# Two attentions in one kernel: the agenda of A's softmax and of B's output weights is rewritten

## The chip, the core and the metric

The kernel runs on one core of a Trainium2 chip. The metric is the device time of one launch in microseconds (us). Before the change three runs took 1605.85, 1606.92 and 1607.03 us; their median, 1606.92, is the time that is compared.

## The reference

Two attention layers work on inputs of 2048 positions by 576 features with 32 heads of 18, in float32, and their outputs are joined along the features.

```python
# A: every position looks at 8 positions, 2 apart, at and behind itself
logits = jnp.einsum("bhsd,bhswd->bhsw", q, kg) * scale
logits = jnp.where(mask, logits, -1e9)
o = jnp.einsum("bhsw,bhswd->bhsd", softmax(logits), vg)
# B: full attention
scores = jnp.einsum("bhqd,bhkd->bhqk", q, k) * scale
o = jnp.einsum("bhqk,bhkd->bhqd", softmax(scores), v)
# both: qkv = x @ wqkv before, o @ wo after
```

## The kernel before

**Stages.** A first part (to about 415 us) projects the inputs with split operands (each float32 number as a high and a low half). Then comes the main loop: B's attention in 512 *steps*, `while step < ALL` (L1272). A step takes one group `g` of four heads, one block `b` of 512 queries and one tile `kt` of 128 keys; 16 steps make a block, 64 a group. Blocks are numbered through, so block 30 is `g` 7, `b` 2 and begins at step 480.

**What a step does.** TensorE (PE) makes four score products (L269), ScalarE (ACT) four exponentials `e` (L277), and PE weighs the values by the exponentials of the step before into `po` (L742, eight matmuls together in a trace, four to a step and two row sets). Beside that PE makes *maximum pieces* for later blocks (L158), score products again, whose row maxima VectorE (DVE) takes (L166): three of them in a step. They go through three PSUM banks in turn, so PE can be at most three pieces ahead of DVE. When a block's 64 pieces are done, DVE reduces and turns them (L176, L183), GpSimd (POOL) splits them into two halves (`halve`, L101 and L102), and `place` (L195) has eight small DMAs write the rows into the tile `qs`, from which the block's own scores are made. A block's first score needs its rows.

**The agenda.** Everything else hangs on a table from steps to closures: `plan(start, ...)` and `later(n, f)` put work on a step, and `due()` issues it, in order, at the end of the step. What is issued is bound to its engine's queue in that order: DVE, POOL and ACT, and SP, which issues nearly all the DMAs, each work strictly through their own queue, so an instruction that waits holds what is behind it.

**A's part.** A is cut into eight pieces `j` of 256 positions; `AT[j]` is the step to which the plan of piece `j` refers (L43, `local`, L891). POOL multiplies queries with shifted keys and adds (`match`, nine times, the last at `AT+25`, which ends in `lg`, L921). DVE takes the maximum over the window (`most`, L932 into `am`, at `AT+31`, 32, 33), POOL subtracts it (`lower`, L938), ACT makes the exponentials (`exponents`, L941, at `AT+35`), DVE adds them (`total`, L932 into `as`, at `AT+36`, 37, 38) and takes reciprocals (`inverses`, L948, at `AT+38` and 39), POOL multiplies (`share`, L951, at `AT+39`) and makes nine weighted sums (`weighted`, L957 to L960, `AT+39` to `AT+59`). The result is split (L964, L969) and stored to `dao` (L972). For the first piece all from `most` on lies three steps earlier. `get` loads it back (L987, L989).

**Double steps.** A's output products for a half tile (288 columns) are put into `inside` at the steps of the table `MADE` (L45). If one stands there when a step with `kt > 0` begins, `together` (L1227) runs two steps as one: eight scores, eight maximum pieces and A's products interleaved over two halves of the array. `due()` for the first of the two is called only after all of this is issued, `due()` for the second after the weighing. There are 32 entries; each stands for one double step that begins one step after it.

**B's results.** When a block is weighed, `finish` (L747) copies `po`, loads its sums of 16 by 128 into `den` one step later, takes their reciprocal (L786) eight steps later, stores it (L787) nine steps later, loads it spread out as `rec` (L788) at 13, multiplies, casts and subtracts on POOL at 20, 21, 22 (L789 to L791) and stores at 26 (L777). The last group has a shorter table.

**B's output weights.** `load_wo` (L849) loads a chunk of rows into a buffer `y` (four buffers, shared with A's outputs), and six steps later POOL splits it into tiles of group 5, free from step 384 on (L101, L102). Chunks 0 to 4 start at steps 455, 457, 459, 461 and 463. The fifth has four pieces of 18 rows and a POOL memset first. `load_wo_stack` (L872) does the like for two stacked pieces at steps 465 and 467, and nine steps later copies rows by DMA (L886). `fetch_old` (L1038) loads 8 transfers of 252 KB: B's results of the seven finished groups for a block of queries, for block 0 at step 452 and for block 1 at step 472.

Of the kernel before, what the change touches and what calls it, by code (L numbers as in the profile page):

```python
# [16 lines left out]
S = 2048  # L17
D = 576
H = 32
DH = 18  # L20
# [19 lines left out]
EARLY_PAIRS = EARLY * NB * PIECES + 2  # L40
AHEAD = 7

AT = [10, 67] + [13 + 55 * j for j in range(2, S // AB)]  # L43

MADE = ((88, 96, 112, 128), (144, 160, 176, 192), (200, 208, 224, 240), (253, 256, 272, 288),  # L45
        (307, 320, 336, 352), (362, 368, 384, 400), (417, 432, 440, 448), (474, 476, 478, 480))


def ap(t, *dims):
# [4 lines left out]
def rows(t, *dims):  # L54

    return bass.AP(tensor=t.tensor, offset=t.offset, ap=[list(d) for d in dims])
# [3 lines left out]
def two_attentions(ctx: ExitStack, tc, xa, wa, woa, xb, wb, wob, out):  # L60
# [686 lines left out]
    def finish(g, b):  # L747
        o = work.tile([128, 512], F32, name="o", bufs=2)
        if g == NG - 1 and b == NB - 1:
            return closing(b, o, work.tile([128, 512], F32, name="rec", bufs=1))  # L750
        if step + 1 in producing and total - sum(given) >= 8:
            leaving.append(lambda: nc.scalar.activation(o, po, AF.Copy))
        elif step + 1 in producing or sum(given) == total:
            nc.scalar.activation(o, po, AF.Copy)
        else:

            nc.vector.tensor_copy(o, po)
            copied.add(step + 1)
# [12 lines left out]

        if g == NG - 1 and b > 0:
            return shortly(b, o, rec, *room())

        def store():
            if g < NG - 1:
                load(do[:, g, :, 512 * b : 512 * b + 512].rearrange("i p n -> p i n"), parts[2].bitcast(F32))  # L777
            else:
                for i in range(2):
                    load(do[i, g, :, 512 * b : 512 * b + 512], parts[i].bitcast(F32))  # L780
                later(2, lambda: stack_new(b))
                plan(step + 2, full(b))

        times = (1, 8, 9, 13, 20, 21, 22, 26) if g < NG - 1 else (1, 6, 7, 10, 13, 14, 15, 16)
        for at, f in zip(times, (lambda: load(den, o[DH:128:32]),
                                 lambda: nc.vector.reciprocal(den, den),  # L786
                                 lambda: load(drec[g, b].rearrange("i (p n) -> (i p) n", n=16), den),  # L787
                                 lambda: load(rec, rows(drec[g, b], (512, 4), (0, 32), (1, 512))),  # L788
                                 lambda: nc.gpsimd.tensor_mul(o, o, rec),  # L789
                                 lambda: nc.gpsimd.tensor_copy(room()[0], o),  # L790
                                 lambda: nc.gpsimd.tensor_sub(parts[1], o, parts[0]),  # L791
                                 store)):
            later(at, f)
# [52 lines left out]
    producing = set()  # L846
    copied = set()

    def load_wo(k, src, *pieces):  # L849

        raw = work.tile([128, D], F32, name="y", bufs=4)
        n = 0
        if len(pieces) == 4:
            nc.gpsimd.memset(raw, 0.0)
            n = 128
        for at, c0, m in pieces:
            load(raw[at : at + m], src[c0 : c0 + m])
            n = max(n, at + m)
        if k == "a":
            hi = work.tile([128, D], F32R, name="wohi", bufs=5)  # L860
            lo = work.tile([128, D], F32R, name="wolo", bufs=5)
        else:

            c = len(wo.get(k, []))
            hi, lo = (ap(t[:, 0, 0, :] if len(t.shape) == 4 else t[:, 0, :], (1, NB * 1024))[:, D * c : D * c + D]
                      for t in sets[(NG - 3) % 3])
        wo.setdefault(k, []).append((hi, lo))
        later(3 if k == "a" else 6, lambda: split_on(nc.gpsimd, hi[:n], lo[:n], raw[:n]))

    wstack = []  # L870
# [1 line left out]
    def load_wo_stack(p):  # L872

        hi, lo = (ap(t[:, 0, 0, :] if len(t.shape) == 4 else t[:, 0, :], (1, NB * 1024))[:, D * (5 + p) : D * (6 + p)]
                  for t in sets[(NG - 3) % 3])
        raw = work.tile([128, D], F32, name="y", bufs=4)
        nc.gpsimd.memset(raw, 0.0)
        for r in range(2):
            load(raw[64 * r : 64 * r + 3 * DH], rows(wob[DH * (H - 4 + r + 2 * p)], (0, 3), (D, DH), (1, D)))
        wstack.append(hi)  # L880
        later(6, lambda: split_on(nc.gpsimd, hi[:118], lo[:118], raw[:118]))

        def middle():
            for r in range(2):
                at = slice(64 * r + DH, 64 * r + 2 * DH)
                load(hi.bitcast(F32)[at], lo.bitcast(F32)[at])  # L886

        later(9, middle)


    def local(j):  # L891
# [104 lines left out]
            for_two.add(inside[-1])  # L996

        def sums_of_a(h, n, alone=True):
            his, los = zip(*wo["a"])
            w = his[:4], los[:4], his[4], los[4]  # L1000
            cols = slice(288 * h, 288 * h + 288)
            if h == 0:
                st["y"] = ys["a", j, n] = work.tile([128, D], F32, name="y", bufs=4)
            y = st["y"][:, cols]
            both = [halves(r, 0, w, st["x", n], cols, slice(0, 128), True) for r in range(2)]
            if not alone:
                return both, y
            one, two = beside("scores", *both)
            nc.scalar.activation(y, two, AF.Copy)
            behind_scores.append(lambda: nc.vector.tensor_add(y, one, y))  # L1010


        soon = 0 if j else 3
        pieces = [(33, lower), (35, exponents), (39, share), (60, upper), (61, rest), (64, lambda: put(0)), (66, lambda: put(1))]

        pieces[:0] = [(at, lambda f=f, n=n: f(n)) for f, ats in ((most, (31, 32, 33)), (total, (36, 37, 38)),
                                                                (inverses, (38, 39))) for n, at in enumerate(ats)]
        for c in range(DH // 2):
            pieces.append((39 + 5 * c // 2, lambda c=c: weighted(c)))
        pieces = [(at - soon, f) for at, f in pieces]  # L1020
        pieces += [(5 + 5 * c // 2, lambda c=c: match(c)) for c in range(DH // 2)]

# [12 lines left out]

    olds = defaultdict(list)

    def fetch_old(b):  # L1038
        for c in range(4):
            h, n = 7 * c, 126  # L1040
            if b < 2:

                t = sets[(NG - 2) % 3][b]
                o = ap(t[:, c, 0] if b == 0 else t[:, c // 2, 1024 * (c % 2) :], (512, 2), (1, 512))
                o = o[:, 0], o[:, 1]

            elif b == 2:
                o = [work.tile([128, D], F32R, name=nm, bufs=5)[:, :512] for nm in ("wohi", "wolo")]
            elif c < 2:
                o = work.tile([128, 2, 512], F32R, name="pr", bufs=2)  # L1050
                o = o[:, 0], o[:, 1]
            else:
                o = ap(work.tile([128, DH, HALO + SUB], F32R, name="akv", bufs=2), (512, 2), (1, 512))
                o = o[:, 0], o[:, 1]
            for i in range(2):
                first = do[i, h // 4, 32 * (h % 4), 512 * b : 512 * b + 512]
                load(o[i].bitcast(F32)[:n], rows(first, (32 * S, 7), (S, DH), (1, 512)))
            olds[b].append([t[:n] for t in o])
# [140 lines left out]
    for k, src, start, chunks in (  # L1199
        ("a", woa, 28, [[(0, 128 * c, 128)] for c in range(4)] + [[(64 * r, 512, 64) for r in range(2)]]),  # L1200
        ("b", wob, STEPS * (NG - 1) + 7,
         [[(0, 126 * c, 126)] for c in range(4)] + [[(32 * i, 504 + DH * i, DH) for i in range(4)]]),
    ):
        plan(start, [((4 if k == "a" else 2) * c, lambda k=k, src=src, ch=ch: load_wo(k, src, *ch)) for c, ch in enumerate(chunks)])
    for j in range(NJ):
        plan(AT[j], local(j))
    for g in range(1, NG):
        if g > EARLY:
            plan(STEPS * (g - 2) + 1, [(n, f) for n, f in enumerate(stack_loads(g))])
        if g == NG - 1:  # L1210
            plan(STEPS * g, [(4, lambda: fetch_old(0)), (17, lambda: load_wo_stack(0)), (19, lambda: load_wo_stack(1)),
                             (24, lambda: fetch_old(1)), (34, lambda: fetch_old(3)),
                             (38, lambda: fetch_old(2))])
            plan(STEPS * g, [(n, lambda t=t, h=h: partial(t, h)) for n, (t, h) in
                             zip((43, 44, 45, 47, 49, 51), [(t, h) for t in range(3) for h in range(2)])])
# [139 lines left out]
```

## Time and profile before

| | |
|---|---|
| time, median of three | 1606.92 us |
| the profiled execution's own time | 1605.83 us |
| its span, first to last instruction | 1604.0 us |
| mean granted TensorE clock | 0.998 |
| busy share of the span: PE, DVE, ACT, POOL | 99%, 85%, 76%, 60% |
| the chain that ended last, by engine | PE 91%, DVE 3%, DMA 2%, ACT 2%, POOL 1%, issue 1% |
| DMA | 175.66 MB, 110 GB/s over the span |

How to read it: a row of the timeline has the start in us from the span's first instruction, the duration, the engine (PEld is PE's weight load, SPq and POOLq the queues that issue DMAs), the line, the operation, `out<-in` by the program's names, the shapes and how many instructions are merged in it. In brackets stands the engine's idle time before it and what ended it. A row of the waits has who waited `<-` for whom, the sum in us, the count and the longest. A row of the chain has the start, the time and what was on the path. A row of the windows has a stretch, its length, each engine's busy time and count, the granted clock, the busy share of 16 DMA engines and GB/s. Matmuls are pipelined and their ends modelled, so a busy PE is not yet PE at its pace.

### The profile page before, as it was taken

How to read it: one execution, taken by the hardware profiler on the slowest of the kernel's cores; microseconds unless marked ns; L12 is line 12 of the kernel's file. 1: busy time of each engine (PE TensorE's matmuls, PEld its weight loads, DVE VectorE, ACT ScalarE, POOL GpSimd, SP SyncE). 2: the span in 40 equal slices, each digit the busy share in tenths (PEclk: the TensorE clock that was granted, in tenths of full speed). 3: DMA queues.
4: the chain of work that ended last, by engine and by line, in shares of the span. 5: the costliest groups of instructions: out<-in, count | busy, mean ns of one | idle time of the engine just before them, and what ended most of it. 6: DMA issues, size and time to landing. Idle time of an engine off the chain costs nothing.

```text
span 1604.0 us, 34970 instructions
## 1 busy us (share of the span) xinstructions
PE 1585.2 (99%) x13276; PEld 963.5 (60%) x13276; DVE 1363.6 (85%) x2315; ACT 1215.1 (76%) x2438; POOL 965.2 (60%) x798
## 2 busy tenths in 40 slices
PE   9999999999999999999999999999999999998998
PEld 7999888999543444444445444445445445545676
DVE  5199999999999999999999999999999999896522
ACT  7323441121699999999999999999999999996655
POOL 2305742210266994995896896897896797791000
PEclk9999999999999999999999999999999999999999
DMA  9837954532221362254326335332632231154311
GB/s 264 224 125 196 273 167 130 146 105 80 60 55 50 83 155 67 52 125 96 73 80 146 77 88 119 96 87 54 135 100 66 61 98 36 51 166 153 120 62 60
DMA packets 188025, 175.66 MB, mean 110 GB/s; under 512 B 119416, under 2 KB 133240, under 8 KB 186128
## 3 DMA queue, kind: packets, MB, share of 16 engines
q1 hardware_dynamic: 182992, 161.88, 36.7%
q0 software_dynamic: 4032, 10.63, 3.1%
q8 instruction: 104, 1.70, 0.5%
q10 hardware_dynamic: 832, 0.92, 0.2%
q14 instruction: 65, 0.53, 0.1%
HBM read 98.77 MB, written 73.47 MB: 107 GB/s over the span
## 4 chain that ended last, share of the span: by engine, by line
PE 91%; DVE 3%; DMA 2%; ACT 2%; POOL 1%; issue 1%; SPq 0%; POOLq 0%; DVEq 0%
PE po L742 28%; PE bank L269 18%; PE bank L158 17%; PE bank L364 16%; PE bank L301 5%; PE bank L1120 4%; PE bank L1245 3%; DVE mx L166 3%; ACT e L277 1%; DMA den<-o 1%; DMA rec<-drec 1%; POOL xlo L412 1%; PE bank L516 0%; ACT lg L941 0%; DMA out<-y 0%
## 5 line engine op out<-in xcount | busy, mean ns | idle before, releaser
L166 DVE TENSOR_REDUCE mx<-bank 128x2 f32<-128x512 f32 x2048 | 1279.8, 683 | 132.8 <-PE bank L158 100.2
L277 ACT ACTIVATE e<-bank 128x512 f32<-128x512 f32 x2048 | 1047.5, 607 | 72.6 <-PE bank L269 66.4
L158 PE MATMUL bank<-ks,qs 54*128 54x512 f32 (+1 forms) x2466 | 791.7, 382 | 4.5 <-DVE mx L166 3.0
L158 PEld LDWEIGHTS bank<-ks,qs 54*128 54x128 f32 x2466 | 404.5, 184 | 387.8 <-DVE mx L166 339.4
L269 PE MATMUL bank<-qs,ks 56*128 56x512 f32 x2048 | 597.4, 426 | 6.6 <-DMA qs<-mt 6.6
L742 PE MATMUL po<-e,v 128*19 128x512 f32 x4096 | 531.4, 598 | 0.0
L269 PEld LDWEIGHTS bank<-qs,ks 56*128 56x128 f32 x2048 | 309.7, 185 | 37.8 <-ACT e L277 24.6
L914 POOL TENSOR_TENSOR pr<-aq,akv 128x1024 f32<-128x1024 f32 x72 | 158.4, 2201 | 15.7 <-DMA akv<-da 12.9
L957 POOL TENSOR_TENSOR pr<-lg,akv 128x1024 f32<-128x1024 f32 x72 | 158.4, 2200 | 0.6
L742 PEld LDWEIGHTS po<-e,v 128*19 128x19 f32 x4096 | 73.8, 97 | 138.4 <-issue 132.9
L918 POOL TENSOR_TENSOR pr<-pr 128x1024 f32<-128x1024 f32 x64 | 152.5, 2383 | 5.0
L692 ACT ACTIVATE ohi<-bank 128x512 f32<-128x512 f32 (+1 forms) x56 | 30.4, 595 | 149.2 <-issue 98.5
L364 PE MATMUL bank<-xhi,ahi 64*128 64x512 f32 (+1 forms) x448 | 114.4, 387 | 0.0
L364 PE MATMUL bank<-xhi,alo 64*128 64x512 f32 (+1 forms) x448 | 110.5, 387 | 0.0
L364 PE MATMUL bank<-xlo,ahi 64*128 64x512 f32 (+1 forms) x448 | 107.7, 388 | 0.1
L1245 PE MATMUL bank<-wohi,at 64*128 64x288 f32 x480 | 103.5, 305 | 0.0
L958 POOL TENSOR_TENSOR pr<-pr 128x512 f32<-128x512 f32 x72 | 92.5, 1284 | 5.6
L1245 PEld LDWEIGHTS bank<-wohi,at 64*128 64x128 f32 x480 | 74.7, 184 | 27.6 <-ACT e L277 23.8
L412 POOL TENSOR_TENSOR alo<-raw,ahi 128x512 fp32r<-128x512 f32 (+1 forms) x14 | 17.5, 1253 | 121.0 <-ACT ahi L411 99.4
L504 POOL TENSOR_TENSOR olo<-olo,ohi 128x512 fp32r<-128x512 f32 x36 | 46.0, 1292 | 61.3 <-ACT ohi L503 55.5
L1245 PE MATMUL bank<-wolo,at 64*128 64x288 f32 x240 | 70.0, 292 | 0.0
L364 PEld LDWEIGHTS bank<-xhi,ahi 64*128 64x128 f32 (+1 forms) x448 | 64.6, 182 | 3.5
(202 smaller groups left out, 1793.9 us busy)
## 6 DMA issues: line engine op xcount, KB each, us to landing
do<-n SPq DMA_DIRECT2D x30, 512.0 KB
da<-ohi SPq DMA_DIRECT2D x52, 256.0 KB
akv<-da SPq DMA_DIRECT2D x64, 175.5 KB
out<-y SPq DMA_DIRECT2D x32, 288.0 KB
qs<-dqk SPq DMA_DIRECT2D x30, 288.0 KB
ks<-dqk SPq DMA_DIRECT2D x30, 288.0 KB
at<-dao SPq DMA_DIRECT2D x60, 128.0 KB
rec<-drec SPq DMA_DIRECT2D x29, 256.0 KB
```

The lines of the kernel that those rows point to most:

```text
L158: return nc.tensor.matmul(ps if part is None else ps[:, 256 * r : 256 * r + 256], qs[at, b, p, 128 * t : 128 * t + 128], ks[at, p, 512 * k ...
L166: nc.vector.tensor_reduce(at, ps.rearrange("q (s n) -> q s n", s=2), axis=AX.X, op=ALU.max)
L269: nc.tensor.matmul(ps, ks[at, p, 128 * kt : 128 * kt + 128], qs[at, b, p], start=True, stop=True)
L277: nc.scalar.activation(e, ps, AF.Exp, scale=SCALE)
L301: nc.tensor.matmul(ps, a, b, start=c == i == 0, stop=c == 4 and i == 1)
L364: nc.tensor.matmul(ps, a, b, start=start, stop=stop)
L742: nc.tensor.matmul(po[32 * i : 32 * i + 19], vs[g][:, kt, 19 * i : 19 * i + 19], es[i], start=kt == 0, stop=kt == NT - 1)
L914: nc.gpsimd.tensor_mul(pr, ap(st["q"][:, 2 * c], (SUB, 2), (0, W), (1, SUB)), window(st["k"], c))
L918: nc.gpsimd.tensor_add(st["pr"], st["pr"], pr)
L957: nc.gpsimd.tensor_mul(at, ap(st["lg"], (0, 2), (SUB, W), (1, SUB)), window(st["v"], c))
L958: nc.gpsimd.tensor_add(at[:, :, :4], at[:, :, :4], at[:, :, 4:])
L1245: return nc.tensor.matmul(ps, a, b, start=r == k == 0, stop=r == 1 and k == len(both[1]) - 1)
```

## The change

`AT` moves four of the eight pieces of A, one by three steps later, three by one or two steps earlier, and `MADE` moves four lone double steps (88 to 101, 200 to 212, 253 to 266, 362 to 376; the other shifts only reorder) so that for seven pieces `AT+35` is the first step of a double step. The reciprocals of A's sums, `share` and the first weighted sum move one step later. In `finish` the reciprocal of the sums, its store and the load of `rec` move from 8, 9, 13 to 10, 11, 14. The fifth weight chunk moves from step 463 to 421, the two stacked pieces from 465 and 467 to 423 and 425; where a memset comes first, the loads are issued three steps after it. `fetch_old(1)` is cut in two halves and moves from step 472 to 458 and 462.

```diff
-AT = [10, 67] + [13 + 55 * j for j in range(2, S // AB)]
+AT = [10, 67, 126, 178, 232, 286, 342, 398]
-MADE = ((88, 96, 112, 128), (144, 160, 176, 192), (200, 208, 224, 240), (253, 256, 272, 288),
-        (307, 320, 336, 352), (362, 368, 384, 400), (417, 432, 440, 448), (474, 476, 478, 480))
+MADE = ((96, 101, 112, 128), (144, 160, 176, 192), (208, 212, 224, 240), (256, 266, 272, 288),
+        (307, 320, 336, 352), (368, 376, 384, 400), (417, 432, 440, 448), (474, 476, 478, 480))
...
-        times = (1, 8, 9, 13, 20, 21, 22, 26) if g < NG - 1 else (1, 6, 7, 10, 13, 14, 15, 16)
+        times = (1, 10, 11, 14, 20, 21, 22, 26) if g < NG - 1 else (1, 6, 7, 10, 13, 14, 15, 16)
...
         if len(pieces) == 4:
             nc.gpsimd.memset(raw, 0.0)
             n = 128
+            later(3, fetch)
...
-            load(raw[64 * r : 64 * r + 3 * DH], rows(wob[DH * (H - 4 + r + 2 * p)], (0, 3), (D, DH), (1, D)))
+            later(3, lambda r=r: fetch(r))
...
-        pieces = [(33, lower), (35, exponents), (39, share), (60, upper), (61, rest), (64, lambda: put(0)), (66, lambda: put(1))]
+        pieces = [(33, lower), (35, exponents), (40, share), (60, upper), (61, rest), (64, lambda: put(0)), (66, lambda: put(1))]
...
-                                                                (inverses, (38, 39))) for n, at in enumerate(ats)]
+                                                                (inverses, (39, 40))) for n, at in enumerate(ats)]
-            pieces.append((39 + 5 * c // 2, lambda c=c: weighted(c)))
+            pieces.append((max(40, 39 + 5 * c // 2), lambda c=c: weighted(c)))
...
+    plan(423, [(0, lambda: load_wo_stack(0)), (2, lambda: load_wo_stack(1))])
...
-            plan(STEPS * g, [(4, lambda: fetch_old(0)), (17, lambda: load_wo_stack(0)), (19, lambda: load_wo_stack(1)),
-                             (24, lambda: fetch_old(1)), (34, lambda: fetch_old(3)),
+            plan(STEPS * g, [(4, lambda: fetch_old(0)), (10, lambda: fetch_old(1, 0, 2)), (14, lambda: fetch_old(1, 2, 4)),
+                             (34, lambda: fetch_old(3)),
                              (38, lambda: fetch_old(2))])
```

The rest of the diff gives `load_wo` the chunk's number, since the fifth chunk now comes first, and puts its transfers into an inner function.

More of the change, by code (lines that the diff above doesn't have):

```diff
@@ L847, in two_attentions, with load_wo, fetch @@
     copied = set()
-    def load_wo(k, src, *pieces):
+    def load_wo(k, src, c, *pieces):
         raw = work.tile([128, D], F32, name="y", bufs=4)
         n = 0
+        def fetch():
+            for at, c0, m in pieces:
+                load(raw[at : at + m], src[c0 : c0 + m])
         if len(pieces) == 4:
@@ L855, in load_wo @@
             n = 128
-        for at, c0, m in pieces:
-            load(raw[at : at + m], src[c0 : c0 + m])
-            n = max(n, at + m)
+            later(3, fetch)
+        else:
+            n = max(at + m for at, c0, m in pieces)
+            fetch()
         if k == "a":
@@ L862, in load_wo @@
         else:
-            c = len(wo.get(k, []))
             hi, lo = (ap(t[:, 0, 0, :] if len(t.shape) == 4 else t[:, 0, :], (1, NB * 1024))[:, D * c : D * c + D]
                       for t in sets[(NG - 3) % 3])
-        wo.setdefault(k, []).append((hi, lo))
+        wo.setdefault(k, {})[c] = hi, lo
         later(3 if k == "a" else 6, lambda: split_on(nc.gpsimd, hi[:n], lo[:n], raw[:n]))
@@ L877, in load_wo_stack, with fetch @@
         nc.gpsimd.memset(raw, 0.0)
+        def fetch(r):
+            load(raw[64 * r : 64 * r + 3 * DH], rows(wob[DH * (H - 4 + r + 2 * p)], (0, 3), (D, DH), (1, D)))
         for r in range(2):
-            load(raw[64 * r : 64 * r + 3 * DH], rows(wob[DH * (H - 4 + r + 2 * p)], (0, 3), (D, DH), (1, D)))
+            later(3, lambda r=r: fetch(r))
         wstack.append(hi)
@@ L998, in sums_of_a @@
         def sums_of_a(h, n, alone=True):
-            his, los = zip(*wo["a"])
+            his, los = zip(*(wo["a"][c] for c in range(5)))
             w = his[:4], los[:4], his[4], los[4]
@@ L1036, in two_attentions, with fetch_old @@
     olds = defaultdict(list)
-    def fetch_old(b):
-        for c in range(4):
+    def fetch_old(b, start=0, end=4):
+        for c in range(start, end):
             h, n = 7 * c, 126
@@ L1203, in two_attentions @@
     ):
-        plan(start, [((4 if k == "a" else 2) * c, lambda k=k, src=src, ch=ch: load_wo(k, src, *ch)) for c, ch in enumerate(chunks)])
+        plan(start, [((4 if k == "a" else 2) * c if len(ch) < 4 else 421 - start, lambda k=k, src=src, c=c, ch=ch: load_wo(k, src, c, *ch))
+                     for c, ch in enumerate(chunks)])
+    plan(423, [(0, lambda: load_wo_stack(0)), (2, lambda: load_wo_stack(1))])
     for j in range(NJ):
```

## The prediction

> **What bounds the kernel now.** First the page's busy shares, to see which engine has no time left, then what PE waits for.
>
> ```profile
> span 1604.0 us, 34970 instructions
> ## 1 busy us (share of the span) xinstructions
> PE 1585.2 (99%) x13276; PEld 963.5 (60%) x13276; DVE 1363.6 (85%) x2315; ACT 1215.1 (76%) x2438; POOL 965.2 (60%) x798
> ```
>
> ```profile
> PE bank L269 <- DMA qs<-mt: 6.6, 1, 6.6
> ```
>
> PE always has work, so a change pays only where PE is held up or falls below its pace. The one large wait is a score product that waits for the rows `place` writes. The next table has four pairs of stretches, each between the starts of two weighings of `po` in PE's timeline, with nearly the same work of PE in a pair (counts differ by missing records): the double steps at 479 and 481; three single steps with A's exponentials (piece 4, step 268) and three without; piece 7's double step, which holds its exponentials, and one that holds none; a single step before and one with DVE's wait for `den`.
>
> ```profile
> 1459.45:1474.10 14.65, 8.08 (x60) 6.19 (x59) 5.79 (x10) 5.20 (x11) 3.13 (x3) 0.77 0.37 130
> 1474.10:1480.12 6.02, 6.02 (x60) 4.29 (x59) 4.33 (x9) 4.04 (x9) 0.00 (x0) 1.00 0.46 167
> 994.85:1001.38 6.53, 6.53 (x50) 2.53 (x48) 6.23 (x12) 6.53 (x15) 0.93 (x1) 1.00 0.72 177
> 705.20:711.30 6.10, 6.10 (x54) 2.59 (x56) 5.77 (x11) 6.09 (x14) 5.96 (x4) 1.00 0.39 98
> 1361.26:1366.24 4.98, 4.98 (x41) 1.99 (x40) 4.12 (x10) 4.49 (x11) 0.00 (x0) 1.00 0.53 119
> 1398.35:1403.34 4.99, 4.99 (x42) 2.00 (x41) 3.58 (x7) 4.00 (x10) 4.75 (x5) 1.00 0.31 94
> 739.74:741.76 2.02, 2.02 (x18) 0.85 (x17) 1.48 (x3) 2.02 (x5) 1.25 (x1) 1.00 0.60 83
> 741.76:744.92 3.16, 2.08 (x18) 0.84 (x16) 2.36 (x5) 2.06 (x5) 2.28 (x5) 1.00 0.13 43
> ```
>
> A single step takes 6.10 / 3 = 2.03 us. The double with step 480, the first of block 30, takes 14.65 - 6.02 = **8.6 too long**; PE idles 6.6 of it, and the other 2.0 come behind the wait, when its granted clock is low (third from the end):
>
> ```profile
> 1465.00:1470.00 5.00, 0.67 (x5) 0.70 (x7) 0.00 (x0) 0.00 (x0) 3.13 (x3) 0.67 0.24 88
> 1470.00:1475.00 5.00, 5.00 (x40) 4.16 (x41) 3.36 (x5) 3.77 (x7) 0.00 (x0) 0.64 0.54 173
> ```
>
> Why the rows were late stands in the timelines of POOL and SP and in the chain.
>
> ```profile
> 1454.86 0.21 POOL L101 CAST mh<-mt 128x32 fp32r<-128x32 f32 x1 [3.29 <-DVE mt L183]
> ```
>
> ```profile
> 1444.93 6.20 SPq L1057 DMA_DIRECT2D ks<-do  x8
> 1451.24 1.48 SPq L777 DMA_DIRECT2D do<-n  x1
> 1452.77 1.18 SPq L788 DMA_DIRECT2D rec<-drec  x1
> 1454.05 4.77 SPq L886 DMA_DIRECT2D qs<-ks  x4
> 1459.60 6.08 SPq L195 DMA_DIRECT2D qs<-mh  x4
> 1465.78 2.18 SPq L195 DMA_DIRECT2D qs<-mt  x4
> ```
>
> ```profile
> 1452.77 12.38 DMA rec<-drec
> 1467.45 1.53 DMA qs<-mt
> ```
>
> POOL casts the rows at 1454.9, but SP was still issuing the copies of the stacked weights (L886). `place` began at 1459.6 and crept, since the eight loads of 252 KB (L1057) were still under way: `rec`, issued behind them, took 12.38 us to land.
>
> **Part 1: weights and old results moved.** In the changed kernel L1057 is issued at 458 and 462 and L886 at 432 and 434, so between `rec` (474) and `place` (478) SP has nothing. `place` can start with POOL, at 1455.1; at 2.18 for four its eight issues take 4.4, the last starts at 1459.0 and lands 1.53 later, at 1460.5. PE asks for the rows inside the double that follows the weighing at 1459.45, not before 1461.3. So the wait is gone, with a margin of about an us: **-8.6**. What the moved steps issue is three memsets, casts and subtractions on POOL and 12 small transfers on SP. The nearest rows:
>
> ```profile
> 1427.83 0.58 POOL L854 MEMSET y<- 128x576 f32 x1
> 1428.35 0.67 POOL L101 CAST qs<-y 126x576 fp32r<-126x576 f32 x1
> 1429.10 1.42 POOL L102 TENSOR_TENSOR ks<-y,qs 126x576 fp32r<-126x576 f32 x1
> ```
>
> ```profile
> 1355.70 1.29 POOL L938 TENSOR_TENSOR lg<-lg,am 128x512 f32<-128x512 f32 x1 [5.48 <-DVE am L932]
> ```
>
> That is 3 x 2.67 = 8.0 us of POOL at steps 421 to 431, where POOL idles 5.5 us before the last piece's `lower` and again behind it: I cost it at nothing. Only the first memset (0.58) goes ahead of the last `match`; without cover DVE would wait that long. On SP the fetches that wait for a memset hold `drec` by a few us, which no one on PE's path awaits. The halves of `fetch_old(1)` put 2 MB ahead of A's last `dao` stores and `get`s; at nothing too, and a rival below.
>
> **Part 2: exponentials in double steps.** By the table three steps with A's exponentials take 6.53 instead of 6.10: 0.43. Pieces 1 to 6 move, piece 0 stays in a single step, piece 7 stood in a double already, and that takes 4.98 beside 4.99 without. So nothing is paid there; I keep 0.05 each. 6 x 0.43 - 0.3 = **-2.3** (between -2.6 and -2.0).
>
> **Part 3: reciprocals.** The step with the wait for `den` takes 3.16 instead of 2.02, and DVE had waited 1.2 (the row at 742.45 of its timeline):
>
> ```profile
> 742.45 0.25 DVE L786 RECIPROCAL den<-den 128x16 f32<-128x16 f32 x1 [1.23 <-DMA den<-o]
> 884.00 0.35 DVE L948 RECIPROCAL as<-as 128x32 f32<-128x32 f32 x1
> ```
>
> So a us that DVE waits is nearly a us of PE. Two steps, 4.1 us, remove it: **-1.1**. The sums' last addition and first reciprocal (0.35) no longer stand in one step. DVE has little room in a step (5.77 of 6.10 busy), so the gain lies between nothing and 0.35 for each of the eight pieces; some meet a `den` instead. I take a quarter: **-0.7**.
>
> **Part 4: POOL, the cost.** `share` waits for the second reciprocal, and from there to the `lg` of the next piece POOL is full: 96.84 of 100.5 us and 96.69 of 100.3, the rest being the pauses of 0.08 between instructions.
>
> ```profile
> 764.90:865.40 100.50, 100.44 (x827) 48.30 (x827) 91.27 (x152) 95.52 (x190) 96.84 (x70) 1.00 0.37 91
> 1007.60:1107.90 100.30, 100.30 (x819) 47.34 (x820) 91.11 (x152) 95.89 (x191) 96.69 (x70) 1.00 0.28 74
> ```
>
> The first stretch runs from piece 2's `share` to the end of piece 3's `lg`, the second from piece 4's to piece 5's. What comes ahead of `share`, and when DVE asks for `lg`:
>
> ```profile
> 764.90 1.29 POOL L951 TENSOR_TENSOR lg<-lg,as 128x512 f32<-128x512 f32 x1 [12.85 <-DVE as L948]
> ```
>
> ```profile
> 776.04 1.27 POOL L789 TENSOR_TENSOR o<-o,rec 128x512 f32<-128x512 f32 x1
> ```
>
> ```profile
> 773.53 1.89 DVE L166 TENSOR_REDUCE mx<-bank 128x2 f32<-128x512 f32 x3 [0.17 <-PE bank L158]
> ...
> 869.88 0.42 DVE L932 TENSOR_TENSOR am<-lg 128x256 f32<-128x256 f32 x1
> ```
>
> Now piece 2's second reciprocal stands at 166 instead of 162, just before the row at 773.53, which is step 167: `share` starts at 773.9, 9.0 later. The multiplication (776.04) and cast of `finish`, 2.0 together, come to stand ahead of it; POOL has 98.5 to do and ends at 872.4. DVE asks at step 209 as before, but the double at 201 has moved behind that step, and a double takes 6.02, 2.0 more than two singles: 869.9 - 2.0 = 867.9. DVE waits 4.5 us where it had 4.5 to spare. Of that I take off 0.8 that it idles there anyway: **+3.7** by part 3's rate. For piece 5:
>
> ```profile
> 1103.34 3.91 DVE L166 TENSOR_REDUCE mx<-bank 128x2 f32<-128x512 f32 x6 [0.15 <-PE bank L158]
> 1107.40 1.89 DVE L166 TENSOR_REDUCE mx<-bank 128x2 f32<-128x512 f32 x3 [0.15 <-PE bank L158]
> 1109.21 0.41 DVE L932 TENSOR_TENSOR am<-lg 128x256 f32<-128x256 f32 x1
> ```
>
> `share` of piece 4 stays at 272. DVE asks two steps earlier (317), in the middle of the row at 1103.34, at 1105.2; `lg` ends at 1107.9, or 0.6 before that since a split of rows falls behind it: a wait of 2.1, PE loses **+1.8**. Piece 4, by the same count, comes out about even: **+0.3**. Behind the waiting DVE stand the row maxima, and PE has three banks before it stops. Together +5.8, not below 0 (POOL early enough after all), at most 7.
>
> **Sum.** -8.6 - 2.3 - 1.1 - 0.7 + 5.8 = -6.9. The profiled execution took 1605.83 (its span of 1604.0 and 1.8 around it) and would take 1598.9; the median lies 1.1 above it: **1600.0**.
>
> **The rivals.** (1) *POOL is not late*, because something in its row is shorter or done earlier than counted. For it: a wait that I infer and no row shows; against it: a row with no gap. 1600.0 - 5.8 = 1594.2. Chance 0.24. (2) *The wait at step 480 stays in part*: the margin is an us, and `place` follows twelve `get`s, a store and `rec` on SP. 6 to 8.6 come back: 1606.0 to 1608.6. Chance 0.14. (3) *The clock falls at piece 3 too* and costs 2.0 as it did at 1470: 1602.0. The 0.64 stood behind 6.6 us of idling, after the 1.2 us of part 3 it was 1.00; 3.7 lies between. Chance 0.05. The Trainium skill, TensorE: Matmul & The Clock Gate, Part 1, has the clock fall to half after an idle window of about 3.4 us that runs free of the kernel; both rows agree, and by that rule this wait is just long enough to do it now and then. (4) *Slower*: the halves of `fetch_old(1)` hold up the last `dao` stores. Eight such loads, a store and `rec` (2.75 MB) needed 1444.93 to 1465.15, 20.2 us. Now the loads share their time with two `dao` stores, the store, `rec` and two weight chunks, 4.5 MB from 1421: at that rate 33 us, to 1454. `get` waits for the stores, its first half lands at about 1457; PE wants it in the double at 475, two doubles of 6 before 1461.3, at 1449.3, waits 8 and pays 2.0 for the clock: 1610.0. It decides from the second store landing after 1446. Against it: 173 GB/s in the window above, with such loads, and SP could reach the stores at about the time it did. Chance 0.07. The Trainium skill, DMA: Bandwidth & Descriptors, in the section on why a DMA increments its semaphore by 16, lets a transfer use the largest number of engines up to 16 that divides both outer sizes, so seven for these rows of 7 x 18. A DMA share of 0.54 in that window agrees roughly; by the rule the stores would queue on those seven.
>
> **How the numbers follow.** The forecast has 0.50, the rivals what is named. About 0.2%, 3.2 us, is what a measurement can tell from no change. Faster by more: the forecast, (1) and (3), less a tail of 0.04: 0.75. Within: (2) and the tail, 0.18. Slower: (4), 0.07. The range goes from just below (1) to the near end of (2): 1593 to 1606.
>
> **What would show it.** Right: no wait of PE for `qs<-mt`, a full clock to the end, `place` issued within an us of POOL's cast; three steps around each of pieces 1 to 6's exponentials without the 0.43; no wait for `den`; DVE waiting at L932 for `lg` of pieces 3 (about 4) and 5 (about 2). Wrong: PE waiting for `at` at step 475, or no wait at L932.

## The result and the profile after

The changed kernel takes **1616.84 us** (median of 6 runs, 1614.27 to 1620.41) beside 1606.52 of the kernel before on the same chip (6 runs, 1605.81 to 1609.69): a ratio of 1.0065, 95% interval 1.0055 to 1.0075. It is slower, where the prediction had 1600.0 and 0.75 on faster. The profiled execution has an own time of 1615.91. First its page.

```profile
span 1614.1 us, 34977 instructions
...
PE 1588.0 (98%) x13276; PEld 968.3 (60%) x13276; DVE 1366.4 (85%) x2315; ACT 1216.0 (75%) x2438; POOL 965.6 (60%) x798
```

The span is 10.1 longer, PE is busy 2.8 longer: most of the time is idling of PE. Its waits, before and then after (who waited `<-` for whom: sum, count, longest):

```profile
PE bank L158 <- DVE mx L166: 3.0, 8, 1.1
```

```profile
PE bank L158 <- DVE mx L166: 11.3, 11, 5.3
PE bank L1256 <- DMA at<-dao: 4.9, 2, 4.4
```

The wait for `qs<-mt` is gone as forecast, but PE now waits for A's output rows `at`, and far longer for DVE, which frees its banks. From L890 on the lines are 9 to 11 higher than before (L930 is the old L921, L941 the old L932, L1256 the old L1245). What DVE waited for, in two stretches of its waits, from 1110 and from 1450 us:

```profile
DVE am L941 <- POOL lg L930: 2.6, 1, 2.6
```

```profile
DVE den L786 <- DMA den<-o: 5.5, 1, 5.5
```

The windows, cut between weighings of `po` as in the prediction: the single step with the old wait for `den`; the double step at 209; the two single steps in which DVE waits for piece 5's `lg`; the step at 471 and the next; the double with step 480 and the one behind it.

```profile
741.29:743.31 2.02, 2.02 (x18) 0.84 (x16) 1.84 (x4) 2.02 (x6) 2.02 (x2) 1.00 0.57 219
861.85:874.59 12.74, 7.89 (x54) 6.36 (x52) 5.86 (x10) 5.78 (x13) 10.04 (x5) 0.73 0.74 157
1113.74:1118.53 4.79, 2.09 (x18) 0.84 (x17) 2.71 (x6) 2.06 (x6) 2.46 (x4) 1.00 0.01 1
1118.53:1121.61 3.08, 3.08 (x18) 1.49 (x16) 2.38 (x6) 2.52 (x6) 1.28 (x1) 0.60 0.06 11
1454.18:1462.33 8.15, 2.85 (x18) 1.49 (x16) 2.74 (x6) 2.48 (x6) 3.13 (x3) 0.68 0.49 131
1462.33:1465.09 2.76, 2.76 (x18) 0.87 (x16) 1.50 (x3) 1.60 (x4) 0.00 (x0) 0.72 0.73 165
1478.35:1484.40 6.05, 6.05 (x61) 4.32 (x60) 4.88 (x10) 4.39 (x10) 1.89 (x2) 1.00 0.48 163
1484.40:1490.42 6.02, 6.02 (x61) 4.29 (x60) 4.84 (x10) 4.37 (x10) 0.00 (x0) 1.00 0.41 140
```

The two doubles at the end run at pace (14.65 before, now 6.05). Each of the three stretches with a wait is long twice over: PE idles, and the granted clock (third from the end) falls to 0.60 to 0.73 behind it.

With the end of every fourth exponential in ACT's timeline as the end of a step, the difference to before adds up so:

| stretch (steps) | after minus before, us | what lies there |
|---|---|---|
| first part | +2.0 | no edit touches it; 415.4 before, 417.4 after, 416.1 to 420.0 in the profiles below |
| 0 to 150 | -0.5 | exponentials of piece 1, reciprocals |
| 150 to 156 | -1.2 | wait for `den` at 153 |
| 156 to 250 | +7.3 | double step at 209 |
| 250 to 300 | +0.3 | piece 4 |
| 300 to 330 | +3.4 | steps 317 to 320 |
| 330 to 468 | +0.6 | small, spread |
| 468 to 474 | +6.8 | wait for `den` at 471 |
| 474 to 511 | -8.7 | wait at step 480 |

**Step 209.** The chain of waits names what ended the stretch (start, time, what); the second row is from the chain around step 471.

```profile
859.75 8.67 DMA at<-dao
```

```profile
1448.41 10.59 DMA den<-o
```

The transfer of `at` was issued at 859.75. SP's timeline, after and then before:

```profile
831.88 0.33 SPq L981 DMA_DIRECT2D dao<-aohi  x1
...
847.66 5.19 SPq L195 DMA_DIRECT2D qs<-mt  x4
...
856.58 0.93 SPq L996 DMA_DIRECT2D at<-dao  x2
857.60 1.46 SPq L998 DMA_DIRECT2D ahl<-dao  x1
859.11 2.81 SPq L996 DMA_DIRECT2D at<-dao  x2
```

```profile
832.16 0.93 SPq L987 DMA_DIRECT2D at<-dao  x2
```

Two things made this `get` 24 us later. `get(0)` of piece 2 hangs on the first entry of its row of `MADE`, eight steps ahead of it: with 200 moved to 208 it went from step 192 to 200, and steps 193 to 204 issue a 288 KB load of stacked rows each (L140, L141). And POOL, late from its `share` on, gave out the halves that `put` stores so late that SP stood at the store, with everything behind it:

```profile
SPq L981 <- POOL aohi L973: 11.9, 1, 11.9
```

POOL's own rows are where the prediction put them (`share` at 773.9, `lg` ending at 872.4):

```profile
773.76 1.28 POOL L960 TENSOR_TENSOR lg<-lg,as 128x512 f32<-128x512 f32 x1 [13.20 <-DVE as L957]
```

```profile
870.92 1.27 POOL L930 TENSOR_TENSOR lg<-pr 128x512 f32<-128x512 f32 x1
```

So DVE's wait for `lg` should have stood at step 209 too; no row shows it, since PE was waiting for `at` at the same time and gave DVE nothing to do.

**Step 471.** SP's timeline shows what was issued just ahead of the load of `den`:

```profile
1440.62 5.43 SPq L1066 DMA_DIRECT2D ks<-do  x4
...
1448.41 0.59 SPq L785 DMA_DIRECT2D den<-o  x1
```

The second half of `fetch_old(1)` took 5.4 us to issue, and the 8 KB of `den` landed 10.6 after their issue, behind 252 KB loads. DVE's reciprocal, which in the last group stands at its old step, waits for them, and the row maxima stand behind it.

### The profile page after: what moved, and what is told of

Read it like the earlier page. It is cut to its first block, busy times and chain, and to the rows that moved or that the text cites. A ratio compares the mean times of both kernels' runs of the same rounds, so it can differ in the third digit from the quotient of the medians.

```text
span 1614.1 us, 34977 instructions
## 1 busy us (share of the span) xinstructions
PE 1588.0 (98%) x13276; PEld 968.3 (60%) x13276; DVE 1366.4 (85%) x2315; ACT 1216.0 (75%) x2438; POOL 965.6 (60%) x798
## 4 chain that ended last, share of the span: by engine, by line
PE 78%; POOL 12%; DVE 4%; DMA 3%; issue 1%; ACT 1%; SPq 0%; POOLq 0%; DVEq 0%; ACTq 0%
PE po L742 23%; PE bank L269 15%; PE bank L158 14%; PE bank L364 14%; PE bank L301 5%; PE bank L1129 4%; DVE mx L166 3%; PE bank L1256 3%; POOL pr L966 2%; POOL pr L923 2%; POOL pr L927 2%; POOL pr L967 1%; POOL pr L968 1%; DMA dqk<-olo 1%; DMA den<-o 1%
## 5 line engine op out<-in xcount | busy, mean ns | idle before, releaser
L1256 PE MATMUL bank<-wohi,at 64*128 64x288 f32 x480 | 105.4, 309 | 4.9 <-DMA at<-dao 4.9
L1256 PEld LDWEIGHTS bank<-wohi,at 64*128 64x128 f32 x480 | 76.1, 188 | 33.2 <-ACT e L277 23.3
L412 POOL TENSOR_TENSOR alo<-raw,ahi 128x512 fp32r<-128x512 f32 (+1 forms) x14 | 17.6, 1256 | 121.3 <-ACT ahi L411 98.8
L101 POOL CAST mh<-mt 128x32 fp32r<-128x32 f32 x32 | 6.7, 210 | 112.4 <-DVE mt L183 112.4
L1256 PE MATMUL bank<-wolo,at 64*128 64x288 f32 x240 | 70.7, 295 | 0.0
```

The costliest lines, as they stand in the source:

```text
L1256: return nc.tensor.matmul(ps, a, b, start=r == k == 0, stop=r == 1 and k == len(both[1]) - 1)
```

## The experiments

Each kernel is the one before or the changed one with the edit shown. Times are medians; the kernel before took 1606.93 beside E1 to E4, 1607.02 beside E6 to E9, 1607.46 beside E5 and E10 to E12. A difference to the changed kernel's 1616.84 compares runs of different groups, between which the kernel before differs by up to 0.9. Since the first part varies by some us from profile to profile, profiles are compared by the *loop*, from the end of step 0 to the end of the span: 1188.6 before, 1196.7 after.

### Which part costs: E1 to E3

E1 (x1_weights_and_old): the changed kernel, with A's tables, A's steps and the times of `finish` as before.

```diff
-AT = [10, 67, 126, 178, 232, 286, 342, 398]
+AT = [10, 67] + [13 + 55 * j for j in range(2, S // AB)]
...
-        times = (1, 10, 11, 14, 20, 21, 22, 26) if g < NG - 1 else (1, 6, 7, 10, 13, 14, 15, 16)
+        times = (1, 8, 9, 13, 20, 21, 22, 26) if g < NG - 1 else (1, 6, 7, 10, 13, 14, 15, 16)
```

> The weight loads and the two halves of fetch_old(1) alone, moved as in the change; A's table, the double steps and the times of den as before. Theory (the halves fill the DMA engines just before den of block 28 is loaded, and DVE waits for it at step 470): the wait of 8.6 us at step 480 goes, a wait of DVE for den of about 5 us comes, which costs 6.9: together 1.7 us faster than before (0 to 3.5). Rival (den at step 470 is late because A's part has put SP behind): no wait for den, 8.6 faster.

E2 (x2_a_alone): the kernel before with the change's `AT`, `MADE`, `share`, `weighted` and `inverses`, and nothing else.

```diff
+AT = [10, 67, 126, 178, 232, 286, 342, 398]
...
-(39, share)
+(40, share)
```

> A's part alone: AT, MADE, share and the reciprocals one step later. Theory (A's new spacing makes POOL and SP late at three places, steps 209, 264 and 317, worth 8.0, 1.2 and 4.2, and the covered exponentials give 2.6 back): 10.8 us slower than before (9 to 12.5), the wait at step 480 stays. Rival (the wait at 209 comes only together with the other parts, A's own cost is what the prediction counted, 5.8 less 3.0): 2.8 slower.

E3 (x3_den_alone): the kernel before with the change's times of `finish`.

```diff
+        times = (1, 10, 11, 14, 20, 21, 22, 26) if g < NG - 1 else (1, 6, 7, 10, 13, 14, 15, 16)
```

> The reciprocal of den, its store and the load of rec two, two and one step later, nothing else. Theory: the one wait of DVE for den at step 153 goes, 1.1 us faster, which the profile shows better than the times. Rival (den is now late somewhere else, or collides with A's reciprocals): 0 to 1 slower.

Measured: E1 1604.98 (ratio 0.9992, 0.9982 to 1.0001), E2 1616.73 (1.0063, 1.0048 to 1.0078), E3 1606.66 (0.9996, 0.9986 to 1.0006). E1's waits have no `qs<-mt`, but the new one for `den`; E2's have the old wait of PE at step 480 and the one for `at`:

```profile
DVE den L786 <- DMA den<-o: 4.8, 1, 4.8
```

```profile
PE bank L269 <- DMA qs<-mt: 7.7, 1, 7.7
PE bank L158 <- DVE mx L166: 5.2, 7, 2.5
PE bank L1245 <- DMA at<-dao: 3.7, 2, 3.3
```

So the wait at 471 comes with the weights and old results, and gives back most of what the end wins (-8.7 and +7.4 in E1's profile; by its times E1 can't be told from no change). A's part costs about 10 us by itself. (In E2's profile the stretch of step 209 loses 5.2, not 7.3: PE's wait for `at` is 1.1 shorter; the rest stays open.) E3's times show no gain, though their interval, down to 0.9986, would hold the 1.1 us that were expected. Moreover E1 and E2, which keep the old times, do not show the wait at step 153 either (their steps 150 to 156 are as short as those of the changed kernel): the 1.2 us of the profile before belong to that execution, in which `den` landed late, as much as to the step of the reciprocal.

### The wait at 471, and what freed step 480: E4 and E5

E4 (x4_old_at_490) and E5 (x13_old_at_472) are the changed kernel with `fetch_old(1)` whole and later, at 490 and at its old step 472.

```diff
-(10, lambda: fetch_old(1, 0, 2)), (14, lambda: fetch_old(1, 2, 4)),
+(42, lambda: fetch_old(1)),
```

> The changed kernel with fetch_old(1) in one piece at step 490, far behind den, get and place. Theory (the halves alone make den late): the wait for den at step 470 goes, the wait at 480 does not come back: 6.9 us faster than the changed kernel, about 3.5 slower than before. Rival A (SP is late because of the weights and drec): the wait for den stays, no gain. Rival B (the early old results were what freed place): the wait at 480 comes back and the gain is under 2.

```diff
-(10, lambda: fetch_old(1, 0, 2)), (14, lambda: fetch_old(1, 2, 4)),
+(24, lambda: fetch_old(1)),
```

> The changed kernel with fetch_old(1) whole at step 472, as before the change; the weights stay early. Theory (den at step 471 waits behind the early old results, and place at step 480 needs them out of its way): DVE's wait for den at step 471 goes (-6.9), but of the wait for qs at step 480 some 2 to 6 come back, since eight loads of 252 KB are still under way when place writes: between 1612 and 1616. Rival (the copies of the stacked weights alone made the rows late): no wait at step 480, 1609 to 1610.

E4 took 1607.62 (1.0005, 0.9995 to 1.0014), 9.2 less than the changed kernel (its loop 8.5 less, 6.8 of it at step 471); no wait at 471, none at 480. E5 took 1609.55 (1.0014, 1.0004 to 1.0023): here the rival came nearer. The wait at 480 comes back as 1.0 us of PE, not 2 to 6, though the eight loads go out just ahead of `place` as before the change:

```profile
PE bank L269 <- DMA qs<-mt: 1.0, 1, 1.0
```

```profile
1453.25 6.23 SPq L1066 DMA_DIRECT2D ks<-do  x8
...
1466.22 2.28 SPq L195 DMA_DIRECT2D qs<-mh  x4
1468.60 4.92 SPq L195 DMA_DIRECT2D qs<-mt  x4
```

```profile
1465.98 0.21 POOL L101 CAST mh<-mt 128x32 fp32r<-128x32 f32 x1 [17.05 <-DVE mt L183]
```

```profile
1470.57:1477.90 7.33, 6.31 (x61) 4.35 (x60) 5.37 (x10) 4.54 (x10) 3.19 (x3) 1.00 0.25 89
```

`place` still creeps (7.3 us for its eight), but it begins 0.2 after POOL's cast, where before the change it began 4.7 after it, behind the copies of the stacked weights (L886). The last row, the window of the double with step 480, is 1.3 over 6.05. Moving the stacked weights, and with them those copies, was worth all but 1.3 of the 8.6; moving the old results was worth the 1.3 and cost 6.8.

### The two causes at step 209: E6 and E7

E6 (x5_get_at_193) is the changed kernel with only that `get` ahead of the stacked loads.

```diff
-pieces.append((ends[0] - 8 if not n else
+pieces.append((193 - AT[2] if j == 2 and not n else ends[0] - 8 if not n else
```

> The changed kernel, with one transfer moved: the first get of piece 2 (at<-dao) is issued at step 193, ahead of the twelve stack loads, instead of step 200, among them. Theory (two waits lie over each other at step 209: PE's for at, and under it DVE's for POOL's late lg): PE's wait for at goes, but DVE's wait for lg comes to light, since lg still ends at about 872 while DVE asks at about 868: the double step at 209 still loses 3.5 to 5, so 3 to 4.5 us are won, about 1612 to 1613.5. Rival (POOL's lateness harms only by holding SP, the wait for lg is hidden by DVE's slack): the whole 8 go, about 1608.5 to 1609.

E7 (x6_piece2_at_123) leaves the `get` behind them and has piece 2 back at its old step.

```diff
-AT = [10, 67, 126, 178, 232, 286, 342, 398]
+AT = [10, 67, 123, 178, 232, 286, 342, 398]
```

> The changed kernel with piece 2's agenda back at step 123 (so its share, its dao stores and piece 3's lg are as early as before the change; its exponentials stand in single steps again, +0.43); the get of piece 2 stays at step 200, among the stack loads. Theory 1 (the place of the get behind the stack loads is enough by itself): PE's wait for at stays at 3 us or more, at most 4 us are won. Theory 2 (the late POOL held SP at the dao stores, and that made the get late): the stores leave at their steps, the get lands in time, and so does lg: 7 to 8 us are won, about 1609.

E6 took 1612.92 (1.004, 1.0025 to 1.0055), 3.9 less; E7 1608.26 (1.0005, 0.9996 to 1.0014), 8.6 less. In E6 PE has no wait for `at`, and DVE's wait for `lg` comes to light:

```profile
DVE am L941 <- POOL lg L930: 4.2, 1, 4.2
```

The windows of E6 and then E7 for the double at 209 and for the second single behind it with the next double:

```profile
862.00:867.15 5.15, 5.15 (x53) 4.04 (x51) 5.11 (x10) 4.93 (x11) 4.99 (x3) 1.00 0.86 207
870.02:882.36 12.34, 8.79 (x69) 5.44 (x68) 8.60 (x18) 7.13 (x15) 3.75 (x3) 0.86 0.54 143
```

```profile
860.92:866.12 5.20, 5.20 (x53) 4.05 (x51) 5.14 (x10) 4.97 (x11) 5.04 (x3) 1.00 0.78 195
868.99:876.30 7.31, 7.31 (x69) 5.00 (x68) 7.31 (x16) 7.03 (x15) 1.29 (x1) 1.00 0.47 131
```

The late `lg` alone costs 12.34 - 7.31 = 5.0; with the late `at` over it the double at 209 alone lost 12.74 - 5.20 = 7.5. They overlap: mending the `get` alone wins 7.5 - 5.0 = 2.5 at that place. (E6's profiled execution was its slowest, 1616.25, with 1.4 more lost at step 317 and 1.8 more at 471 than the changed kernel's, so its whole loop says nothing.) In E7 one cause is taken away, POOL's lateness, and both waits go. The place of the `get` behind the stacked loads is harmless by itself: SP reached it at 849.47 in E7 (856.58 after the change), and it was in time.

```profile
849.47 0.93 SPq L996 DMA_DIRECT2D at<-dao  x2
```

### Step 317: E8

E8 (x7_piece5_at_288) is the changed kernel with piece 5 back at its old step.

```diff
+AT = [10, 67, 126, 178, 232, 288, 342, 398]
```

> The changed kernel with piece 5's agenda back at step 288 (before the change's place; its exponentials stand in single steps again, +0.43). Theory (at 286 DVE asks for piece 5's lg two steps before POOL has it): DVE's wait of 2.6 at L941 goes, the steps 317 to 320 come back to their pace, -4.2 + 0.4, about 1613. Rival (DVE's wait is covered by the banks and the slow steps have another cause): no more than 1 us is won.

It took 1613.37 (1.0039, 1.0024 to 1.0054), 3.5 less. The windows of two single steps and the double behind them, after and E8:

```profile
1113.74:1127.24 13.50, 10.80 (x86) 6.45 (x84) 9.90 (x19) 9.13 (x19) 4.12 (x6) 0.87 0.16 43
```

```profile
1114.23:1123.58 9.35, 9.35 (x86) 5.85 (x84) 9.21 (x17) 9.12 (x20) 2.57 (x2) 1.00 0.25 63
```

4.15 for a wait of 2.6: the rest is the clock at 0.60 in the step behind it. The same wait costs other amounts in other executions. E4's stretch, and E6's, which had a wait of 2.7:

```profile
1114.23:1126.27 12.04, 9.32 (x85) 5.81 (x83) 9.90 (x19) 9.13 (x19) 3.74 (x5) 1.00 0.16 39
```

```profile
1110.98:1125.83 14.85, 12.11 (x85) 7.11 (x84) 9.99 (x19) 9.13 (x19) 5.68 (x7) 0.77 0.15 40
```

In E4 the clock stayed at 1.00 and the place lost 2.7; in E6 it lost 5.5. So what the clock adds to a wait of this length lay between nothing and about 3 us.

### The good parts alone, and all three waits mended: E9 to E12

E9 (x9_end_and_den) is the kernel before with the early weights, the times of `finish`, and `fetch_old(1)` at 490; A is untouched.

```diff
+        times = (1, 10, 11, 14, 20, 21, 22, 26) if g < NG - 1 else (1, 6, 7, 10, 13, 14, 15, 16)
...
+    plan(423, [(0, lambda: load_wo_stack(0)), (2, lambda: load_wo_stack(1))])
...
+(42, lambda: fetch_old(1)),
```

> The kernel before, with the changed times of finish (10, 11, 14), the early fifth chunk and stacked weights, and fetch_old(1) whole at step 490; A's agenda is as before the change. Theory (the terms add): the wait at step 480 goes (-8.6), the wait for den at step 153 goes (-1.1), no wait for den at step 471 comes: -9.7, about 1597. Rival (without the early fetch something else, the later fetch_old(1) behind the end of the loop, takes the gain back): 1603 or more.

E10 (x10_covered) is E9 with four lone double steps on the exponentials that `AT` of before gives, and the `get` of piece 2 held at 192.

```diff
-MADE = ((88, 96, 112, 128), (144, 160, 176, 192), (200, 208, 224, 240), (253, 256, 272, 288),
-        (307, 320, 336, 352), (362, 368, 384, 400), (417, 432, 440, 448), (474, 476, 478, 480))
+MADE = ((96, 101, 112, 128), (144, 160, 176, 192), (208, 212, 224, 240), (256, 267, 272, 288),
+        (307, 320, 336, 352), (368, 377, 384, 400), (417, 432, 440, 448), (474, 476, 478, 480))
...
+pieces.append((192 - AT[2] if j == 2 and not n else ends[0] - 8 if not n else
```

> The kernel before with the changed times of finish, early weights, fetch_old(1) at step 490, and four lone double steps moved onto the exponentials of pieces 1, 3, 4 and 6 (102, 213, 268, 378) while the pieces' agenda and the get of piece 2 stay where they were. Theory (0.43 for each set of exponentials that comes into a double step, and no new wait, since POOL is as early as before): 1.7 less than the same kernel without the moved double steps (1598.5): about 1596.8. Rival (a lone double step moved behind DVE's wait for lg brings that wait two us nearer and costs as much): 1598 to 1600.

E11 (x11_mended) is the changed kernel with the edits of E4, E7 and E8 together; E12 (x12_piece4_at_233) is E11 with piece 4 a step later.

```diff
+AT = [10, 67, 123, 178, 232, 288, 342, 398]
```

> The changed kernel with its three waits taken away at once: fetch_old(1) whole at step 490, piece 2's agenda at 123, piece 5's at 288 (their exponentials in single steps again). Theory (three waits with separate causes, whose prices add): -9.2 - 8.6 - 3.5 from the changed kernel's 1616.8, about 1595.5, 11 below the kernel before. Rival (what is won at one place is lost at the next, since POOL and SP are full): 1600 or more.

```diff
+AT = [10, 67, 123, 178, 233, 288, 342, 398]
...
+(256, 267, 272, 288)
```

> The kernel of the run before in this call with piece 4's agenda one step later (233, its lone double step at 267), so that DVE's am of piece 4 starts some 2 us later. Theory (am took 1.49 us instead of 0.42 because POOL's multiplication of finish, L789, ran beside it and DVE had to wait for its end): am ends 0.2 to 0.4 after whichever two-input POOL operation runs when it starts; if none does it takes 0.42 and the step at 264 costs 1.2 less. Rival (am is long because of what DVE waits for in lg): it stays at 1.5 whatever runs on POOL. In time about the same as the run before, within 1.5.

E9 took 1598.50 (0.9944, 0.9928 to 0.9961), 8.5 less than before where 9.7 were expected, **E10 1596.12 (0.9929, 0.9914 to 0.9944)**, the fastest, E11 1598.69 (0.9947, 0.9932 to 0.9961), E12 1602.78 (0.9969, 0.9957 to 0.9980). E10's page, for comparison with PE's 1585.2 before:

```profile
span 1594.5 us, 34971 instructions
...
PE 1582.3 (99%) x13276; PEld 966.6 (61%) x13276; DVE 1364.4 (86%) x2315; ACT 1214.8 (76%) x2438; POOL 965.2 (61%) x798
```

E10's loop is 2.1 shorter than E9's (1177.5 and 1179.6), without a new wait, but not all of it belongs to the exponentials. E9's profile loses 0.8 in two steps from 886.2 on, where an addition of piece 3 ran beside POOL's multiplication and took 1.20 instead of 0.28 (rows of DVE and POOL):

```profile
883.65 1.20 DVE L941 TENSOR_TENSOR as<-as 128x128 f32<-128x128 f32 x1
```

```profile
883.41 1.29 POOL L789 TENSOR_TENSOR o<-o,rec 128x512 f32<-128x512 f32 x1 [6.19 <-DMA at<-dao]
```

Neither the kernel before nor E10 has that. Against the kernel before, E10's stretches around the four moved double steps (steps 86 to 106, 197 to 218, 251 to 273, 359 to 384) are 0.3, 0.65, 0.5 and 0.3 shorter: 0.4 for each set of exponentials. E11's median is 3.2 above the expected sum; its loop (1179.6) is 17.1 below the changed kernel's, and the three edits one by one took 8.5, 7.6 and 1.5 from it, 17.6, so there the prices add. (E8's 1.5 is less than the 4.15 at its place: its double at 209 lost 1.4 more, and its steps 368 to 400 1.0, most of it where `am` of piece 6 ran beside POOL's multiplication and took 1.26 instead of 0.41. E11 has 0.9 of the latter, with an `am` of 1.07.) What makes the rest of the 3.2 in the medians stays open; the first part, which no edit touches, took 420.0 in E11's profile, the longest of all. E12 missed its expectation by 2.6: its steps 321 to 323 took 13.0 instead of 8.2 in E11. Piece 4's `share`, and with it POOL's `lg` of piece 5, came a step later there, and DVE waited 3.3 us for it.

E12's question was the length of `am`. The rows of DVE and of POOL, of the changed kernel and then of E12:

```profile
993.80 1.49 DVE L941 TENSOR_TENSOR am<-lg 128x256 f32<-128x256 f32 x1
```

```profile
993.72 1.28 POOL L789 TENSOR_TENSOR o<-o,rec 128x512 f32<-128x512 f32 x1
```

```profile
987.73 1.42 DVE L941 TENSOR_TENSOR am<-lg 128x256 f32<-128x256 f32 x1
```

```profile
987.58 1.30 POOL L791 TENSOR_TENSOR n<-o,n 128x512 fp32r<-128x512 f32 x1
```

In both, `am` (0.42 where nothing of the kind runs beside it) starts just after a two-input operation of POOL and ends 0.27 to 0.29 after that one's end, whichever it is. E12 only moved `am` from L789 onto L791, so it could not win the 1.2.

## Why the prediction was wrong, point by point

**Part 1, weights and old results.** The wait at 480: forecast -8.6, found -8.7, clock included. "The halves of `fetch_old(1)` ... at nothing" is the first step that failed. Of rival 4 the mechanism was right (2 MB in a queue that something on the path needs) and its place wrong: it looked at `get`, issued nine steps ahead of need, and not at `den`, a load of 8 KB whose reader stands in DVE's queue ahead of PE's row maxima: +6.8, where rival 4 had +10 at step 475. Its test, PE waiting for `at` at step 475, would have missed it. The credit was put on the wrong move as well: E5 shows that the stacked weights, by their copies on SP, held `place`, while the old results could have stayed at a price of 1.3.

**Part 2, the exponentials.** -2.3 forecast. E10 shows 0.4 for each of four in a kernel where A's steps stay, so the 0.43 was right. In the changed kernel they do not stand alone: with the waits taken off (7.6 that E7 wins at step 209, 1.2 of `am`, 4.15 at 317) the table has -0.5 up to step 150, -0.3 in 156 to 250, -0.9 in 250 to 300, -0.7 in 300 to 330 and +0.6 in 330 to 468: -1.8 together with the separated reciprocals, where parts 2 and 3 had -3.0.

**Part 3, the reciprocals.** The wait for `den` at 153 is gone (-1.2 against -1.1), but E1 and E2 lack it with the old times, and E3's times show no gain: the term was read from one execution's landing time, so that the wait is gone is no proof of the step. The separated reciprocals take 0.2 from piece 0's steps (steps 42 to 52: 22.91 after, 23.10 before), within the bounds given.

**Part 4, POOL.** Right in every time it named: `share` 773.76 for 773.9, the end of `lg` 872.19 for 872.4, DVE's wait 4.2 (E6) for 4.5 at piece 3 and 2.6 for 2.1 at piece 5, none at piece 4. Wrong in what it made of them: +5.8, "at most 7", against some 13 (7.6 that E7 wins, 4.15 and 1.2). Three things are missing. *The clock*: a wait was priced at 0.8 to 0.9 us of PE for each us of DVE, the rate of a wait of 1.2 us, after which the clock was still 1.00. (The 3.7 for piece 3 even leaves that rate out: 4.5 - 0.8 at 1.14 for 1.23 are 3.4.) The waits of 2.6 and 4.2 cost 4.15 and 5.0. This was rival 3, given 0.05 and only for piece 3; it held at piece 5 in the changed kernel (in E4 it did not) and at piece 3 in E6. *The stores*: a late POOL also holds the stores it feeds and SP behind them, so that `at` was late and lay over the wait for `lg`: 7.5 instead of 5.0. *The `get`*: its step follows `MADE`; "moves lone double steps" was taken as moving PE's work alone; this hurt only together with the late stores, as E7 shows. A fourth, 1.2 at step 264 (a step of 3.27 instead of 2.05), lies where `am` ran beside POOL's multiplication.

**The rivals.** (1), POOL not late, is refuted; (2), the wait at 480 staying, too. No rival had an unforeseen wait beside the forecast's gains at the end of the loop, and the range ended at 1606, at no loss, because the only slow case had 0.07. Of the 17.0 between the 1598.9 forecast for the profiled execution and its 1615.91, the wait for `den` is 6.8, part 4 some 7, parts 2 and 3 1.2, and 2.0 the scatter of the first part.

## What to carry to other kernels

When a load is moved ahead, list every later transfer in the same queue by the step at which an *in-order engine* reads it, small ones first: 8 KB behind 2 MB stopped DVE, and PE with it. When work moves in a table, search for all that is computed from the table: here a `get` went with the double steps. Price a stall of the busiest engine with the clock behind it, as a range (a wait of 2.6 to 2.7 cost 2.7 to 5.5 here), and read a term off one execution only if a second one shows it too.

## What the runs showed of the hardware

The clock can fall after shorter gaps than the wait of 6.6 had shown. Windows of the changed kernel, behind the waits at 209, 317 and 471:

```profile
866.00:870.00 4.00, 2.24 (x11) 1.79 (x13) 0.88 (x2) 0.60 (x1) 3.84 (x3) 0.57 0.90 202
...
1117.00:1121.00 4.00, 3.50 (x22) 2.02 (x24) 3.30 (x8) 2.41 (x5) 0.75 (x1) 0.77 0.04 8
...
1460.00:1465.00 5.00, 4.46 (x24) 2.22 (x24) 3.24 (x6) 2.47 (x5) 0.88 (x1) 0.61 0.75 170
```

PE idled 4.79 - 2.09 = 2.7 us around 1116, and the step behind it ran at 0.60. The Trainium skill, TensorE: Matmul & The Clock Gate, Part 1, names an idle window of about 3.4 us as what brings the clock down; here 2.7 was enough, so the measurement decides, and a gap under that figure is not safe. Nor is it sure to cost: in E4 PE idled 12.04 - 9.32 = 2.7 us at the same place, and the clock stayed at 1.00.

A maximum or an addition of DVE on two SBUF operands waited for the end of POOL's two-input operation beside it: `am` took 1.42 to 1.49 us instead of 0.42, and in E9 an addition of half that size 1.20 instead of 0.28. The Trainium skill, SBUF — State Buffer, in the section on SBUF's two separate sides, says that such a DVE operation and a GpSimd operation that reads SBUF share a port pair which the first to start holds to its end. The three pairs of rows above agree, and so do the first maximum and the first addition of every piece in all 14 traces, 224 rows of 128x256: the 168 with no operation of POOL beside them took 0.41 to 0.43 us, while 31 took 0.83 to 1.50, and each of these ended 0.28 or 0.29 us after an operation of POOL that had begun before it (30 with two inputs, one a cast). A memset of POOL, which reads nothing, was running when 11 others began, and they took 0.41 to 0.43. No experiment took POOL's operation away and left the rest as it was.
